# Attention and MLP block on one core: leftover parts of a half unit go to the next dense group, GpSimd's share of the normalisation written as a sum and a product, memsets and weight pieces spread out

## The chip, the cores and the metric

The kernel runs on one core of a Trainium2 chip. The metric is the device time of one execution in microseconds. Before the change it is 1500.49 us, the median of 3 runs (1500.31 to 1501.24).

## The reference

A transformer layer with both branches fed by the same normalised rows. 2048 rows of 512 numbers; 32 heads of 16; a hidden layer of 1792.

```
x  = A_x                                   # 1 x 2048 x 512, fp32
xn = (x - mean(x)) / sqrt(var(x) + 1e-5)   # per row
q, k, v = split(xn @ wqkv)                 # 32 heads of 16
p  = softmax(q k^T / 4)
out = x + (p v) @ wo + gelu(xn @ w1 + b1) @ w2 + b2
```

Everything is fp32 on the outside. Inside, an fp32 operand of a product is kept as two fp16 halves, high and low, and a product is made as three (high·high, high·low, low·high; `PAIRS` in the code). The exps and their product with v stay fp32.

## The kernel before

**Units.** The attention is cut into 512 units: 8 groups of 4 heads, 4 blocks of 512 query columns, 16 steps each. A unit has a score half and an exps half. The score half makes 4 tiles of scores (line 287, four products of 32x512 each, written side by side) and VectorE takes the row maximum of each tile (line 288). The exps half of the same unit comes 20 units later (`LEAD`), since it needs the maxima of all 16 steps: 4 products of q and k again with the maximum folded in (`e_half`), ScalarE's exp on each (line 339), and the fp32 products of the exps with v (`v_half`). So each pass through `unit()` does the score half of unit u and the exps half of unit u - 20.

**Dense work.** The fp32 products with v occupy one half of the rows of the array at a time, and the other half of the rows is given to what the code calls dense groups: sums of products that belong to the projections, the MLP or the output projection. A group is a list of products for each half of the array (side 0 and 1), an accumulation bank, and a `finish` that takes the result out. `dense(gen, side)` puts in so many *parts* (a part is 256 columns of a product; a full product of 512 columns is two) for each half unit, a number called the pace. The pace before is 8 parts for v groups, projections and 5 of 9 of the hidden groups (`FAST`), 6 for the other hidden groups (`SLOW`), and 7 for the groups of the second MLP product (`MEAN`). A hidden group has 24 parts a side, a sum group 42. Only one group is current (`cur[0]`, lane D), and when it ends in a half unit, the share that is left there is not used. A second lane, E, exists already, and is used at the very end only.

**Order of a run.** It is written out by hand at the start and then generated.
- *Start.* x comes in as 16 blocks of 128 rows. `stats(sb)` normalises four blocks: statistics on VectorE (lines 790 and 792), a short chain on `sd`, a 128x4 tile (lines 794 to 805), and then the normalisation of `xs` itself, which VectorE does for the first four blocks (line 815), and of the second four GpSimd for two (line 810), VectorE for one and ScalarE, in two passes, for one; GpSimd does all of the blocks from 8 on. TensorE transposes them (line 834), ScalarE, VectorE and GpSimd split the result into high and low (`xt`, line 842 for GpSimd), and `side(sb, w)` makes the first q and k projections (line 482). `prep_v` prepares v's weights: an absolute maximum on VectorE (line 751), then the split. `clear(i)` fills 16 stacks of q and k with GpSimd's memsets (lines 86 and 87); `clear(1)` stands in the start, ahead of GpSimd's first normalisation.
- *Units 0 to 15*, written as `scores(u, fills...)`: a score half whose spaces are filled with rows of v (`v_rows`, line 591: 12 products of 128x512 for each block of 128 rows), transposes, sides of the projection, and steps of `ms`, which measures the MLP weights by absolute sums on ScalarE (line 756). 9 of the 16 blocks of v are made here; 7 are left for later (`MOVED`).
- *Units 16 to 19* (`LEAD`) with `burst(LFILL)`, full-height products of the dense groups, 3 in each half unit.
- *Units from 20 on*: dense groups in the order v groups, projections of the other three quarters of the heads, hidden groups and sum groups by turns, and the output projection. After unit 511 the exps halves run on for 20 units, and then full-height products end the run.

**Beside it.** `prepare()` scales and splits the 16 pieces of w1, w2 and wo on GpSimd (lines 1038, 1039 and 1040), one piece after another as its queue comes free, and the split pieces go to DRAM. GpSimd's work in the units goes through `pooled`, a queue with an estimate of its load; DMAs and late steps go through `later(n)`, which runs a step n half or whole slots on. SyncE issues every DMA, in program order, so what stands behind a waiting DMA waits too. The loads of the q and k stacks (line 439) go there, and so do the steps of each query block's division: denominators out (line 377), back across partitions (line 380), a reciprocal on VectorE (line 383).

Of the kernel before, what the change touches and what calls it, by code (L numbers as in the profile page):

```python
# [24 lines left out]
NC = D // P  # L25
# [6 lines left out]
FAST, MEAN, SLOW, LATE = (8, 8), (7, 7), (6, 6), 6  # L32
MOVED = 7
# [4 lines left out]
LFILL = 3  # L38
# [11 lines left out]
def layer_kernel(ctx: ExitStack, tc: tile.TileContext, x, wqkv, wo, w1, b1, w2, b2, out):  # L50
# [32 lines left out]
    def clear(i):  # L83
        for b in range(NQB):
            for p in range(2):
                nc.gpsimd.memset(kst[i][p][b].bitcast(F32), MROW2)
                nc.gpsimd.memset(qst[i][p][b].bitcast(F32), 0.0)
# [76 lines left out]

    def split(hi, lo, src, inv):

        nc.scalar.activation(hi, src, AF.Copy, scale=inv)
        nc.vector.scalar_tensor_tensor(lo, src, inv, hi, op0=ALU.mult, op1=ALU.subtract)
# [274 lines left out]
    def dbank():  # L443
        turn[0] += 1
        if pos[0] < LEAD:
            return banks(free[turn[0] % len(free)]), None
# [6 lines left out]
    class Group:  # L453
# [3 lines left out]
        def __init__(self, prods, alloc, finish, ready=None, first=True, last=True, upper=None, pace=FAST):  # L457
# [87 lines left out]
    def project(m, w, sb, wh, bank, early=False, then=lambda: None):  # L545
# [6 lines left out]
        def finish(pj):  # L552
# [6 lines left out]
            if early or (w == 1 and not m):  # L559
# [17 lines left out]
        return Group(prods, bank, finish)  # L577
# [46 lines left out]
    def group(gen, lane=0):  # L624

        if cur[lane] is None and not spent[0]:
            cur[lane] = next(gen, 0)
            if cur[lane] == 0:
                cur[lane], spent[0] = None, True
        return cur[lane]  # L630

    def ended():

        for lane, f in enumerate(cur):
            if f is not None and f.over():
                cur[lane] = None
                f.end()

# [15 lines left out]
    def dense(gen, side, between=lambda: None):  # L654
# [28 lines left out]
    def unit(gen):  # L683
# [4 lines left out]
        if u == LEAD and cur[0] is not None:  # L688
            burst(gen, cur[0].left())
# [40 lines left out]
    with ExitStack() as st1:  # L730
# [55 lines left out]
        def stats(sb):  # L786
# [20 lines left out]
            for i in range(4):  # L807
                v = xs[4 * sb + i]
                if sb > 1 or (sb and i < 2):
                    nc.gpsimd.tensor_scalar(v, v, mv[:, i, 0:1], sd[:, 2, i:i + 1], op0=ALU.subtract, op1=ALU.mult)  # L810
# [534 lines left out]
```

## Time and profile before

| what | value |
|---|---|
| median of 3 runs | 1500.49 us |
| the profiled execution's own time | 1496.13 us |
| span of that execution | 1494.3 us |
| TensorE busy | 1442.6 us, 97% |
| VectorE busy | 1353.4 us, 91% |
| ScalarE busy | 1246.1 us, 83% |
| GpSimd busy | 763.2 us, 51% |
| mean granted clock of TensorE | 0.985 |

The span is what the trace covers; the profiled execution took 1.8 us more than that, and 4.4 us less than the median of the runs. Lines are those of the kernel before unless the text says otherwise. In a list of groups by line stands the operation, what it writes and reads, its tile, how many, the busy time and the mean of one in ns, and the idle time ahead of it with what ended that. In a table of windows stands for each stretch its length, the busy time of TensorE, its weight loads, VectorE, ScalarE and GpSimd (with counts), the granted clock, the busy share of the DMA engines and their GB/s; with a line given, it shows that line's engine alone. Since four maxima of line 288 make a unit, a quarter of their count is the number of units in a stretch.

### The profile page before, as it was taken

How to read it: one execution, taken by the hardware profiler on the slowest of the kernel's cores; microseconds unless marked ns; L12 is line 12 of the kernel's file. 1: busy time of each engine (PE TensorE's matmuls, PEld its weight loads, DVE VectorE, ACT ScalarE, POOL GpSimd, SP SyncE). 2: the span in 40 equal slices, each digit the busy share in tenths (PEclk: the TensorE clock that was granted, in tenths of full speed). 3: DMA queues.
4: the chain of work that ended last, by engine and by line, in shares of the span. 5: the costliest groups of instructions: out<-in, count | busy, mean ns of one | idle time of the engine just before them, and what ended most of it. 6: DMA issues, size and time to landing. Idle time of an engine off the chain costs nothing.

```text
span 1494.3 us, 89118 instructions
## 1 busy us (share of the span) xinstructions
PE 1442.6 (97%) x40674; PEld 945.1 (63%) x40674; DVE 1353.4 (91%) x2302; ACT 1246.1 (83%) x2383; POOL 763.2 (51%) x860
## 2 busy tenths in 40 slices
PE   6698989999999999999999999999999999999998
PEld 3234556667656666666666666666666666676675
DVE  6677989999999999999999999999999999999923
ACT  3256878888988999999999899999899989998874
POOL 5510288943477664665466375476556537541000
PEclk8899999999999999999999999999999999999999
DMA  5464166522332312112111211121111211002332
GB/s 187 125 181 136 56 203 223 185 78 94 103 118 70 88 37 65 34 58 62 51 37 62 78 29 38 44 73 52 57 44 48 69 41 51 16 23 85 111 125 97
DMA packets 117999, 124.50 MB, mean 83 GB/s; under 512 B 28920, under 2 KB 89592, under 8 KB 117620
## 3 DMA queue, kind: packets, MB, share of 16 engines
q1 hardware_dynamic: 117620, 118.79, 25.8%
q8 instruction: 318, 5.21, 1.4%
q14 instruction: 61, 0.50, 0.1%
HBM read 81.00 MB, written 37.60 MB: 79 GB/s over the span
## 4 chain that ended last, share of the span: by engine, by line
PE 88%; POOL 4%; DVE 3%; issue 2%; ACT 2%; DMA 1%; SPq 0%; DVEq 0%; POOLq 0%; ACTq 0%
PE pD L191 25%; PE pV L191 24%; PE pT L191 18%; PE pS L287 16%; PE pS L191 2%; POOL xs L810 1%; PE pT L591 1%; DVE mt L288 1%; ACT pe L339 1%; PE pS L482 0%; POOL t L1127 0%; DMA wq<-in_A_wqkv_dram 0%; POOL g L1129 0%; DMA wch<-in_B_w_dram 0%; POOL xt L842 0%
## 5 line engine op out<-in xcount | busy, mean ns | idle before, releaser
L288 DVE TENSOR_REDUCE mt<-pS 128x1 f32<-128x512 f32 x2048 | 1280.0, 683 | 62.6 <-PE pS L287 42.9
L339 ACT ACTIVATE pe<-pT 128x512 f32<-128x512 f32 x2048 | 1105.0, 598 | 149.0 <-PE pS L287 83.9
L191 PE MATMUL pV<-pe,vv 64*32 64x512 f32 x8192 | 1092.1, 597 | 3.1 <-issue 2.9
L191 PE MATMUL pT<-qst,kst 64*32 64x512 f16 x8192 | 677.2, 377 | 6.2 <-ACT pe L339 2.9
L287 PE MATMUL pS<-kst,qst 62*32 62x512 f16 x8192 | 614.3, 379 | 5.8 <-DVE mt L288 5.4
L191 PE MATMUL pD<-w_s,g 64*32 64x512 f16 (+1 forms) x6144 | 363.6, 348 | 0.1
L191 PE MATMUL pD<-xb,wc 64*32 64x512 f16 x5376 | 361.3, 375 | 0.0
L287 PEld LDWEIGHTS <-qst 62*32 62x32 f16 x8192 | 246.9, 92 | 124.7 <-issue 29.8
L191 PEld LDWEIGHTS <-kst 64*32 64x32 f16 x8192 | 255.0, 93 | 98.1 <-issue 20.8
L191 PEld LDWEIGHTS <-g 64*32 64x32 f16 x6144 | 198.3, 92 | 88.3 <-POOL g L1129 1.5
L191 PEld LDWEIGHTS <-wc 64*32 64x32 f16 x5376 | 174.8, 92 | 83.4 <-issue 0.4
L191 PEld LDWEIGHTS pV<-pe,vv 64*32 64x32 f32 x8192 | 181.1, 105 | 12.0 <-issue 6.8
L191 PE MATMUL pD<-xt,wqk_h 64*32 64x512 f16 x2400 | 161.3, 375 | 3.6 <-issue 3.6
L1156 POOL TENSOR_SCALAR hh<-hh,fac,b_s 128x512 f32<-128x512 f32 x56 | 43.0, 769 | 154.0 <-ACT hh L1154 150.4
L1183 POOL TENSOR_TENSOR xa<-xa,yt 128x512 f32<-128x512 f32 x32 | 41.0, 1283 | 141.4 <-ACT yt L1181 141.4
L191 PEld LDWEIGHTS <-wqk_h 64*32 64x32 f16 x2400 | 78.8, 92 | 36.9 <-issue 6.7
L394 POOL TENSOR_TENSOR osb<-osb,rb 128x512 f32<-128x512 f32 x31 | 39.9, 1286 | 84.9 <-DMA rb<-den_d 82.8
L1127 POOL TENSOR_TENSOR t<-t,hh 128x512 f32<-128x512 f32 x56 | 71.8, 1282 | 4.7
L1134 POOL TENSOR_TENSOR t<-t,hh 128x512 f32<-128x512 f32 x56 | 71.8, 1282 | 4.7
L1129 POOL TENSOR_TENSOR g<-t,g 128x512 f16<-128x512 f32 x56 | 65.2, 1164 | 4.7
L1132 POOL TENSOR_TENSOR t<-hh 128x512 f32<-128x512 f32 x56 | 58.2, 1040 | 4.7
L1220 DVE SCALAR_TENSOR_TENSOR ac<-pS,gs,ac 128x512 f32<-128x512 f32 x19 | 13.3, 746 | 50.0 <-PE pS L191 45.5
(153 smaller groups left out, 960.2 us busy)
## 6 DMA issues: line engine op xcount, KB each, us to landing
wch<-in_B_w_dram SPq DMA_DIRECT2D x28, 512.0 KB
wc<-w_d SPq DMA_DIRECT2D x56, 256.0 KB
qk_d<-stg SPq DMA_DIRECT2D x32, 256.0 KB
rb<-den_d SPq DMA_DIRECT2D x31, 256.0 KB
w_d<-wsp SPq DMA_DIRECT2D x28, 256.0 KB
kst<-qk_d SPq DMA_DIRECT2D x128, 48.0 KB
qst<-qk_d SPq DMA_DIRECT2D x128, 48.0 KB
xs<-in_A_x_dram SPq DMA_DIRECT2D x16, 256.0 KB
```

The costliest lines, as they stand in the source:

```text
L191: p = nc.tensor.matmul(*args, **kw)
L287: nc.tensor.matmul(s[32 * j:32 * j + 32], qs[p][qb][r, c:c + 32], ks[p][kb][r, :], start=True, stop=True)
L288: nc.vector.reduce_max(mt_of[t][:, n, qt, kb:kb + 1], s, axis=AX.X)
L339: nc.scalar.activation(pe, st, AF.Exp, scale=factor(exp_scale, sexp[0:1, g // 2:g // 2 + 1]))
L394: pooled((1280, lambda: nc.gpsimd.tensor_tensor(osb, osb, rb, op=ALU.mult)), (620, lambda: nc.gpsimd.tensor_scalar(ot[:, 0], osb, 1.0, 0.0 ...
L591: nc.tensor.matmul(pj, xt[:, i, c, t * P:(t + 1) * P], wh[j][:, c, :], start=(n == 0), stop=(n == 11))
L1127: (1280, lambda: nc.gpsimd.tensor_tensor(t1, t1, hh, op=ALU.mult)),
L1129: (1160, lambda: nc.gpsimd.tensor_tensor(g[:, 1, f, :], t1, g[:, 0, f, :], op=ALU.subtract)),
L1132: pooled((1040, lambda: nc.gpsimd.tensor_tensor(t1, hh, hh, op=ALU.mult)), (620, lambda: nc.gpsimd.tensor_scalar(t1, t1, 1.0, 1.0 / GELU_A ...
L1134: (1280, lambda: nc.gpsimd.tensor_tensor(t1, t1, hh, op=ALU.mult)),
L1156: later(1, lambda: pooled((690, lambda: nc.gpsimd.tensor_scalar(hh, hh, scale, bias, op0=ALU.mult, op1=ALU.add)), (0, lambda: gelu(hh, g, ...
L1183: add = lambda: nc.gpsimd.tensor_tensor(xa, xa, yt, op=ALU.add)
```

## The change

- **Hand-over.** `pace` is 8 for v groups and projections and 7 for everything else. When a group has nothing left for a side in a half unit, `dense` gives the rest of that half unit's parts to the next group, in the other lane; `lane[0]` says which lane is the current one. 680 products that were 512 columns wide become two of 256.
- **Front of the dense list.** `MOVED` goes from 7 to 6, so that 10 blocks of v are made by hand at the start; `LFILL` goes from 3 to 4; the burst that emptied the current group at unit 20 goes.
- **Normalisation.** GpSimd's form is (x + (-mean))·rstd instead of (x - mean)·rstd, with -mean in a column of `sd` that is there already. The fourth block of the second quarter goes from ScalarE to VectorE.
- **Memsets.** `clear(1)` is spread over units 7 to 15.
- **Order at the start.** The statistics of the second quarter stand ahead of v's absolute maximum on VectorE; 6 instead of 12 products of v stand ahead of unit 0; transposes, sides and stacks of the later quarters stand one or two units later. Sides (1,1), (2,1) and (3,1) are taken out by ScalarE and GpSimd instead of ScalarE and VectorE. The split of v's weights is in two steps.
- **Weight pieces.** Piece n isn't put in before 4·n units after the first.
- **Small moves.** The x of the next MLP block is fetched one slot later, the accumulators of the output projection earlier (`len(acs) - 2` instead of `2 + 2 * len(acs) - 6`).

```
@@ -29 +29 @@
 LEAD = 20
-FAST, MEAN, SLOW, LATE = (8, 8), (7, 7), (6, 6), 6
-MOVED = 7
+FAST, MEAN, LATE = (8, 8), (7, 7), 6
+MOVED = 6
...
 TAIL = 12
-LFILL = 3
+LFILL = 4
@@ -83 +83 @@
             for p in range(2):
+                yield
@@ -454 +448 @@
-        def __init__(self, prods, alloc, finish, ready=None, first=True, last=True, upper=None, pace=FAST):
+        def __init__(self, prods, alloc, finish, ready=None, first=True, last=True, upper=None, pace=MEAN):
@@ -556 +550 @@
             given("act", 600)
-            if early or (w == 1 and not m):
+            if early:
@@ -574 +568 @@
-        return Group(prods, bank, finish)
+        return Group(prods, bank, finish, pace=FAST)
@@ -621 +615 @@
-    def group(gen, lane=0):
-        if cur[lane] is None and not spent[0]:
-            cur[lane] = next(gen, 0)
-            if cur[lane] == 0:
-                cur[lane], spent[0] = None, True
-        return cur[lane]
+    lane = [0]
+    def group(gen, k=0):
+        if cur[k] is None and not spent[0]:
+            cur[k] = next(gen, 0)
+            if cur[k] == 0:
+                cur[k], spent[0] = None, True
+        return cur[k]
+    def busy():
+        return any(f is not None for f in cur)
...
-        for lane, f in enumerate(cur):
+        for k, f in enumerate(cur):
             if f is not None and f.over():
-                cur[lane] = None
+                cur[k] = None
                 f.end()
+        if cur[lane[0]] is None and cur[1 - lane[0]] is not None:
+            lane[0] = 1 - lane[0]
@@ -659 +660 @@
             return
-        f = group(gen)
-        n = 0 if f is None else f.pace[pos[0] % 2]
-        n = some_of(f, side, n, 0 if f is not None and f.ends(n) else BEHIND)
+        f = group(gen, lane[0])
+        if f is None:
+            between()
+            return
+        def share(n, until):
+            n = some_of(f, side, n, until)
+            if n > until and f.left(side) == 0 and (side == 0 or cur[1 - lane[0]] is not None):
+                g = group(gen, 1 - lane[0])
+                if g is not None and (n > 1 or g.at != [0, 0]):
+                    n = some_of(g, side, n, until)
+            return n
+        n = f.pace[pos[0] % 2]
+        n = some_of(f, side, n) if f.ends(n) else share(n, BEHIND)
         between()
-        some_of(f, side, n)
+        share(n, 0)
...
-        for lane, user in enumerate("DE"):
-            leave(user, cur[lane] is not None and not cur[lane].over())
+        for k, user in enumerate("DE"):
+            leave(user, cur[k] is not None and not cur[k].over())
...
             enter()
-            for lane, f in enumerate(cur):
-                while f is not None and f.left((k + lane) % 2):
-                    f.product((k + lane) % 2)
+            for i, f in enumerate(cur):
+                while f is not None and f.left((k + i) % 2):
+                    f.product((k + i) % 2)
@@ -685 +698 @@
         e = u - LEAD
-        if u == LEAD and cur[0] is not None:
-            burst(gen, cur[0].left())
@@ -807 +818 @@
                 if sb > 1 or (sb and i < 2):
-                    nc.gpsimd.tensor_scalar(v, v, mv[:, i, 0:1], sd[:, 2, i:i + 1], op0=ALU.subtract, op1=ALU.mult)
-                elif sb and i == 3:
-                    nc.scalar.activation(v, v, AF.Identity, bias=sd[:, 4, i:i + 1])
-                    nc.scalar.activation(v, v, AF.Copy, scale=sd[:, 2, i:i + 1])
+                    nc.gpsimd.tensor_scalar(v, v, sd[:, 4, i:i + 1], sd[:, 2, i:i + 1], op0=ALU.add, op1=ALU.mult)
@@ -865 +873 @@
             fac_v.append(fac)
-            for i in range(2):
-                cs = slice(i * W, (i + 1) * W)
-                split(wvh[0][:, :, cs], wvh[1][:, :, cs], wvf[i], inv[:, 0:1])
+            halves = [slice(i * W, (i + 1) * W) for i in range(2)]
+            for cs, v in zip(halves, wvf):
+                nc.scalar.activation(wvh[0][:, :, cs], v, AF.Copy, scale=inv[:, 0:1])
+            yield
+            for cs, v in zip(halves, wvf):
+                nc.vector.scalar_tensor_tensor(wvh[1][:, :, cs], v, inv[:, 0:1], wvh[0][:, :, cs], op0=ALU.mult, op1=ALU.subtract)
+                yield
@@ -945 +957 @@
         turn_all(0)
+        run(ln)
+        some(l1, 2)
         run(pq)
-        run(ln)
-        clear(1)
-        some(l1, 2)
-        some(pv, 1)
-        some(l1, 1)
+        some(l1, 4)
...
         run(l1)
+        some(pv, 1)
@@ -962 +973 @@
         free_banks["S"].append(free_banks["T"].pop(0))
-        ln, vs = stats(2), v_rows()
+        ln, vs, rest_0 = stats(2), v_rows(), clear(1)
         pj = side(1, 1)
-        for n in range(3):
-            some(pj, 4)
-            some(pv, 1)
+        some(pj, 4)
+        some(pv, 1)
+        some(ln, 1)
+        some(pj, 4)
+        some(pv, 1)
+        some(ln, 1)
+        some(pj, 3)
+        some(pv, 1)
+        some(ln, 2)
...
         run(pv)
-        some(ln, 5)
...
         run(ln)
-        some(vs, 12)
+        some(vs, 6)
         ln = stats(3)
-        scores(0, (vs, 3), (turn_x(2, 0), 1), (vs, 3), (turn_x(2, 1), 1))
-        for w in (1, 0):
-            stacks(0, w, [1])
+        scores(0, (vs, 10))
+        stacks(0, 1, [1])
+        scores(1, (vs, 3), (turn_x(2, 0), 1), (vs, 3), (turn_x(2, 1), 1))
         some(ln, 2)
-        scores(1, (vs, 3), (turn_x(2, 2), 1), (vs, 3), (turn_x(2, 3), 1))
+        scores(2, (vs, 3), (turn_x(2, 2), 1), (vs, 3), (turn_x(2, 3), 1))
         some(ln, 2)
-        scores(2, (side(2, 1), 13))
-        some(ln, 4)
         fetch(0)
-        scores(3, (side(2, 0), 13))
+        scores(3, (side(2, 1), 13))
         run(ln)
-        scores(4, (vs, 3), (turn_x(3, 0), 1), (ms, 1), (vs, 3), (turn_x(3, 1), 1))
-        for w in (1, 0):
-            stacks(0, w, [2])
-        scores(5, (vs, 3), (turn_x(3, 2), 1), (ms, 1), (vs, 3), (turn_x(3, 3), 1))
-        scores(6, (side(3, 1), 13), (ms, 1))
-        scores(7, (vs, 8), (ms, 1))
-        for u in range(8, 16):
-            scores(u, (vs, 4), (ms, 1), (vs, 4), (ms, 1))
-            if u == 8:
+        scores(4, (vs, 4), (ms, 1), (vs, 4))
+        stacks(0, 0, [1])
+        scores(5, (vs, 3), (turn_x(3, 0), 1), (ms, 1), (vs, 3), (turn_x(3, 1), 1))
+        stacks(0, 1, [2])
+        scores(6, (vs, 3), (turn_x(3, 2), 1), (ms, 1), (vs, 3), (turn_x(3, 3), 1))
+        scores(7, (side(3, 1), 13), (ms, 1), (rest_0, 2))
+        scores(8, (side(2, 0), 13), (ms, 2), (rest_0, 2))
+        for u in range(9, 16):
+            scores(u, (vs, 6 if u < 11 else 5), (ms, 1), (vs, 5), (ms, 1), (rest_0, 1))
+            if u == 9:
                 stacks(0, 1, [3])
-            elif u == 9:
                 wfs.append(load_qk(1))
+            elif u == 10:
+                stacks(0, 0, [2])
         run(vs)
+        run(rest_0)
@@ -1064 +1081 @@
             nc.vector.tensor_scalar_mul(gs[:, 1:2], gs[:, 1:2], 0.5)
-            ended = [True]
+            ended, first = [True], pos[0]
...
                 v = fetch(16 + n)
-                while not ended[0]:
+                while not ended[0] or pos[0] < first + 4 * n:
@@ -1157 +1174 @@
             return Group([lambda c=c, i=i, j=j: (wc[:, i, c, :], xb[:, j, c, :]) for c in range(NC) for i, j in PAIRS],
-                         dbank, hidden, pace=FAST if (HF * s + f) % 9 in (0, 2, 4, 6, 8) else SLOW)
+                         dbank, hidden)
@@ -1167 +1184 @@
             if q == 3 and s % 2 == 0:
-                fetch_x(b + 1)
+                later(1, lambda: fetch_x(b + 1))
@@ -1185 +1202 @@
             return Group([lambda f=f, i=i, j=j: (g[:, i, f, q * P:(q + 1) * P], w2_s[:, j, s % 2 * HF + f, :])
-                          for f in range(HF) for i, j in PAIRS], dbank, store, lambda n: (s, n // 3) in done, pace=MEAN)
+                          for f in range(HF) for i, j in PAIRS], dbank, store, lambda n: (s, n // 3) in done)
@@ -1278 +1295 @@
                     acs[k] = p3.tile([P, D], F32, name=f"ac{k}")
-                    later(2 + 2 * len(acs) - 6, lambda k=k: read_acc(acs[k], k))
+                    later(len(acs) - 2, lambda k=k: read_acc(acs[k], k))
```

VectorE at the start, where the second quarter is normalised (`mv` and `sd` the statistics, `xs` the rows, `stg` a side on its way out, `am_v` the maximum of v's weights); before:

```order
L792 BN_AGGR mv<-bs 128x2
L794 TENSOR_SCALAR sd<-mv 128x4
L751 TENSOR_REDUCE am_v<-wch 128x1
L798 TENSOR_SCALAR sd<-mv 128x4
L799 TENSOR_TENSOR sd<-sd 128x4
L561 TENSOR_TENSOR stg<-pS,stg 128x512
L801 TENSOR_TENSOR sd<-sd 128x4
L803 RECIPROCAL sd<-sd 128x4
L805 SCALAR_TENSOR_TENSOR sd<-sd 128x4
L815 TENSOR_SCALAR xs<-xs,mv,sd 128x512
```

and now:

```order
L803 BN_AGGR mv<-bs 128x2
L805 TENSOR_SCALAR sd<-mv 128x4
L524 TENSOR_TENSOR sexp<-fac_239 128x1
L525 TENSOR_SCALAR sexp<-sexp 128x1
L809 TENSOR_SCALAR sd<-mv 128x4
L810 TENSOR_TENSOR sd<-sd 128x4
L812 TENSOR_TENSOR sd<-sd 128x4
L814 RECIPROCAL sd<-sd 128x4
L816 SCALAR_TENSOR_TENSOR sd<-sd 128x4
L555 TENSOR_TENSOR stg<-pS,stg 128x512
L823 TENSOR_SCALAR xs<-xs,mv,sd 128x512 x2
L762 TENSOR_REDUCE am_v<-wch 128x1
```

The maximum of v's weights and the side's `stg` stood in the middle of the chain on `sd`, and stand behind it now; the block of xs that ScalarE normalised is VectorE's second.

GpSimd at the start, from the last of the memsets on; before:

```order
L86 MEMSET kst_1_3_97 128x256
L87 MEMSET qst_1_3_113 128x256
L810 TENSOR_SCALAR xs<-xs,mv,sd 128x512 x2
L842 TENSOR_TENSOR xt<-pf,xt 128x512 x2
L567 TENSOR_TENSOR stg<-pf,stg 128x512
L810 TENSOR_SCALAR xs<-xs,mv,sd 128x512 x4
L842 TENSOR_TENSOR xt<-pf,xt 128x512 x4
L567 TENSOR_TENSOR stg<-pf,stg 128x512
L810 TENSOR_SCALAR xs<-xs,mv,sd 128x512 x4
```

and now:

```order
L518 TENSOR_TENSOR wqk_h<-wq,wqk_h 128x512
L821 TENSOR_SCALAR xs<-xs,sd 128x512 x2
L850 TENSOR_TENSOR xt<-pf,xt 128x512 x2
L561 TENSOR_TENSOR stg<-pf,stg 128x512 x2
L821 TENSOR_SCALAR xs<-xs,sd 128x512 x4
L850 TENSOR_TENSOR xt<-pf,xt 128x512 x4
L561 TENSOR_TENSOR stg<-pf,stg 128x512
L821 TENSOR_SCALAR xs<-xs,sd 128x512 x4
```

The 16 memsets that stood between `wqk_h` and the first `xs` are gone from here, and one more `stg` stands ahead of the third quarter's `xs`.

GpSimd where the first weight pieces are split, after unit 20 (`wch` a piece, `wsp` its halves, `stg` a projection's result; the numbers tell the pieces apart); before:

```order
L1038 TENSOR_SCALAR wch_2950<-wch_2950,inv3_2660 128x2x4x128
L1039 TENSOR_SCALAR wsp_3155<-wch_2950 128x2x512
L1040 TENSOR_TENSOR wsp_3155<-wch_2950,wsp_3155 128x2x512
L1038 TENSOR_SCALAR wch_2952<-wch_2952,inv3_2660 128x2x4x128
L1039 TENSOR_SCALAR wsp_3353<-wch_2952 128x2x512
L1040 TENSOR_TENSOR wsp_3353<-wch_2952,wsp_3353 128x2x512
L569 TENSOR_SCALAR stg_3447<-pf_3448 128x512
L570 TENSOR_TENSOR stg_3447<-pf_3448,stg_3447 128x512
```

and now:

```order
L1055 TENSOR_SCALAR wch_2075<-wch_2075,inv3_2692 128x2x4x128
L1056 TENSOR_SCALAR wsp_2954<-wch_2075 128x2x512
L1057 TENSOR_TENSOR wsp_2954<-wch_2075,wsp_2954 128x2x512
L563 TENSOR_SCALAR stg_3048<-pf_3049 128x512
L564 TENSOR_TENSOR stg_3048<-pf_3049,stg_3048 128x512
L1055 TENSOR_SCALAR wch_2953<-wch_2953,inv3_2692 128x2x4x128
L1056 TENSOR_SCALAR wsp_3354<-wch_2953 128x2x512
L1057 TENSOR_TENSOR wsp_3354<-wch_2953,wsp_3354 128x2x512
```

Pieces that followed each other directly have a projection's `stg` between them now.

More of the change, by code (lines that the diff above doesn't have):

```diff
@@ L922, in layer_kernel @@
         nc.vector.memset(wvh[0][:, 0, :], 0.0)
-        clear(0)
+        run(clear(0))
         ln, l1, pq, pv = stats(0), stats(1), prep_qk(0, wfs[0], sbank, ready_w), prep_v()
@@ L1100, in layer_kernel @@
         fil, pre, more = rest(), prepare(), True
-        while not spent[0] or more or cur[0] is not None:
+        while not spent[0] or more or busy():
             unit(fil)
@@ L1253, in layer_kernel @@
         fil, spent[0] = mlp(), False
-        while not spent[0] or cur[0] is not None:
+        while not spent[0] or busy():
             more_stacks()
```

9 lines of the change are left out of this document (2 added, 7 removed).

## The prediction

> **What bounds the kernel now.** First the page: the busy time by engine (share of the span, instructions), and the chain of work that ended last, by engine.
>
> ```profile
> PE 1442.6 (97%) x40674; PEld 945.1 (63%) x40674; DVE 1353.4 (91%) x2302; ACT 1246.1 (83%) x2383; POOL 763.2 (51%) x860
> PE 88%; POOL 4%; DVE 3%; issue 2%; ACT 2%; DMA 1%; SPq 0%; DVEq 0%; POOLq 0%; ACTq 0%
> ```
>
> TensorE bounds it, so only two kinds of gain exist: less work on TensorE, or less waiting by it. The chain leaves TensorE for 12% of the span, with 4% on GpSimd. The windows over all engines show where TensorE waits.
>
> ```profile
> 42.50:56.30 13.80, 5.87 (x47) 2.47 (x46) 4.42 (x11) 3.22 (x8) 10.53 (x6) 0.67 0.37 115
> 56.30:68.40 12.10, 11.55 (x100) 4.62 (x89) 10.95 (x25) 5.02 (x11) 4.58 (x4) 0.95 0.25 66
> 68.40:80.20 11.80, 4.91 (x30) 2.05 (x27) 2.45 (x5) 2.24 (x6) 9.44 (x6) 0.62 0.66 213
> 80.20:111.80 31.60, 30.63 (x276) 11.52 (x269) 27.70 (x46) 18.57 (x51) 3.47 (x3) 0.98 0.66 194
> 180.00:300.00 120.00, 112.37 (x3247) 73.78 (x3236) 107.69 (x181) 96.51 (x182) 98.16 (x87) 1.00 0.64 201
> 320.00:385.00 65.00, 65.00 (x1990) 45.81 (x1979) 63.77 (x104) 58.01 (x110) 17.98 (x23) 1.00 0.28 87
> 480.00:1380.00 900.00, 899.17 (x27342) 613.33 (x27332) 880.96 (x1465) 816.22 (x1551) 503.66 (x567) 1.00 0.18 52
> ```
>
> From 480 to 1380 us TensorE is full (899.17 of 900), so the even pace has little to win there. Two stretches of the hand-written start stand out: TensorE idles 13.80 - 5.87 = 7.93 and 11.80 - 4.91 = 6.89 us, GpSimd is busy, and the granted clock falls to 0.67 and 0.62. The third place is 180 to 300 us. Counting the maxima of line 288, four to a unit, gives its pace.
>
> ```profile
> 180.00:300.00 120.00, 102.37 (x162) 1.00 0.64 201
> 320.00:385.00 65.00, 63.25 (x100) 1.00 0.28 87
> 189.70:220.00 30.30, 22.80 (x36) 1.00 0.71 217
> 245.60:300.30 54.70, 48.43 (x76) 1.00 0.58 184
> ```
>
> 180 to 300 us: 162/4 = 40.5 units at 2.96 us; 320 to 385 us: 25 at 2.60. The weight pieces cost 40.5 x 0.36 = 14.7 us.
>
> **A: up to unit 0.** The second quarter's normalisation, in the timeline of several engines:
>
> ```profile
> 17.71 2.22 DVE L794 TENSOR_SCALAR sd<-mv 128x4 f32<-128x4 f32 x1
> 42.26 0.17 DVE L794 TENSOR_SCALAR sd<-mv 128x4 f32<-128x4 f32 x1
> 19.60 0.31 POOL L87 MEMSET qst<- 128x256 f32 x1
> 21.98 4.38 POOL L810 TENSOR_SCALAR xs<-xs,mv,sd 128x512 f32<-128x512 f32 x2 [2.07 <-DVE sd L805]
> 24.36 0.47 PE L834 MATMUL pT<-ident,xs 128*128 128x128 f32 x1 [4.43 <-POOL xs L810]
> ```
>
> The same small operation on `sd` takes 2.22 us here and 0.17 later; here it ends at 19.93, with the last memset (19.91). With the memsets gone: -2.05. The next price is GpSimd's normalisation. The trace has no sum-and-product on `xs`; the nearest row is line 1156, a product and a sum with two columns on a tile of the same size.
>
> ```profile
> L810 POOL TENSOR_SCALAR xs<-xs,mv,sd 128x512 f32<-128x512 f32 x10 | 20.9, 2098 | 2.4 <-DVE sd L805 2.4
> L1156 POOL TENSOR_SCALAR hh<-hh,fac,b_s 128x512 f32<-128x512 f32 x56 | 43.0, 769 | 154.0 <-ACT hh L1154 150.4 <-DMA kst<-qk_d 3.5
> 39.82 2.75 PE L591 MATMUL pT<-wvh,xt 128*128 128x512 f16 x12
> 67.28 1.16 POOL L567 TENSOR_TENSOR stg<-pf,stg 128x512 f16<-128x512 f32 x1 [5.16 <-ACT stg L566]
> ```
>
> I take 0.77 for 2.10, bounded by no change on one side; nothing in the trace suggests less than 0.77. Two of them: 4.38 - 1.54 = -2.84. Six products of v leave the front: 6 x 2.75/12 = -1.4. Against it: VectorE gets another block, and a side now passes through GpSimd (1.16 each); I put +0.8 for what of that isn't covered by TensorE's own projections. A = -2.05 - 2.84 - 1.4 + 0.8 = -5.5. TensorE's first wait for `xs` alone is 4.43, nearly the first two terms together, so they can be had. Range -4 (half of GpSimd's gain) to -6.3 (no +0.8).
>
> **B: units 0 to 15.** Both idle stretches belong to GpSimd's groups of four.
>
> ```profile
> 44.85 8.24 POOL L810 TENSOR_SCALAR xs<-xs,mv,sd 128x512 f32<-128x512 f32 x4
> 68.72 8.24 POOL L810 TENSOR_SCALAR xs<-xs,mv,sd 128x512 f32<-128x512 f32 x4 [0.28 <-DVE sd L805]
> ```
>
> Four take 4 x 0.77 = 3.1 instead of 8.24, which is -5.2 twice; the later place of transposes and sides, with rows of v ahead of them, covers the rest. So the 14.8 us of idle time go, but the sides that now leave through GpSimd (1.16 each, two of them near the third and fourth quarters) can hold up `xs` or `xt`: I leave 2.3. Added: 18 products of v (6 from the front, 12 for the tenth block), 18 x 0.229 = +4.1. Clock: full clock would make 5.87 and 4.91 shorter by 0.33 x 5.87 + 0.38 x 4.91 = 3.8; I take half, since some waits stay: -1.9. The 16 memsets (16 x 0.31 = 5 us) now lie under units 7 to 15, where GpSimd is busy 3.47 of 31.6: nothing. B = -14.8 + 2.3 + 4.1 - 1.9 = -10.3. Range -6 (waits of 6.6 remain) to -13 (no waits, full clock).
> The Trainium skill (TensorE: Matmul & The Clock Gate, Part 1: The HAM clock gate) says that the clock is either half or full, dropping after an idle window of about 3.4 us and returning after about as long of sustained work. The rows agree with a fall after idleness (0.67 and 0.62, against 0.95 between them); as no idle window of that length would remain, the rule would give the whole 3.8, and B = -12.2.
>
> **C: units 16 to 20.** Here ScalarE must finish measuring before the exps start, and its last pieces stand on SyncE behind the maxima of the first block.
>
> ```profile
> 113.57 0.37 SPq L317 DMA_DIRECT2D m_d<-mhl  x1
> 118.01 0.38 SPq L745 DMA_DIRECT2D wch<-in_B_w_dram  x1
> 122.28 0.63 ACT L756 ACTIVATE wch<-wch 128x512 f32<-128x512 f32 x1 [5.46 <-DMA wch<-in_B_w_dram]
> ```
>
> The chain (maxima stored after unit 15, then load, then measure) keeps its order and moves with unit 15. The eight extra products that `LFILL` puts into units 16 to 19 are v's, which otherwise stand later, and fall where TensorE waits for ScalarE anyway: 0, +/-2.
>
> **E: weight pieces.** Pieces now stand 4 units apart at least, 4 x 2.6 = 10.4 us.
>
> ```profile
> 245.00:300.00 55.00, 17.15 (x8) 1.00 0.59 185
> 400.00:415.00 15.00, 15.00 (x452) 9.72 (x437) 14.46 (x24) 14.20 (x29) 8.98 (x10) 1.00 0.46 140
> 216.06 0.39 PE L191 MATMUL pD<-xt,wqk_h 64*32 64x512 f16 x1 [2.06 <-issue]
> ```
>
> The first row is line 1040: 8 pieces in 55 us, 6.9 apart, at a DMA share of 0.59. Spaced, the 0.31 above the quiet 0.28 shrinks to 0.31 x 6.9/10.4 = 0.21, a share of 0.49. At 0.46 (second row, all engines) TensorE has no gap; at 0.58 a unit is 0.28 longer (54.70/19 = 2.88), at 0.71 0.77 longer (30.30/9). On a straight line from 0.46 to 0.58 a share of 0.49 leaves 0.07, and 0.51 would leave 0.12; on 16 x 4 = 64 units that is 4.5 to 7.7 us of the 14.7. Loads of stacks still come in bunches on top, and the gap in the last row is put down to "issue", not to a DMA; so I halve the gain of 7 to 10 to E = -4, range 0 to -9.
>
> **F: unit 123.** The division of a query block comes late (its first DMA stands behind loads of stacks on SyncE's queue) and holds VectorE, then TensorE:
>
> ```profile
> 418.67 0.56 SPq L377 DMA_DIRECT2D den_d<-osb  x1
> 423.48 0.34 DVE L383 RECIPROCAL dn<-dn 64x32 f32<-64x32 f32 x1 [3.21 <-DMA dn<-den_d]
> 424.42 0.40 PE L287 MATMUL pS<-kst,qst 62*32 62x512 f16 x4 [2.88 <-DVE mt L288]
> ```
>
> The MLP, and with it the loads of stacks, begins 4 units earlier, so SyncE is clear by then: -2.88, less a chance that the maxima at unit 116 now queue behind them. F = -2.5, range -3.4 to +1.
>
> **G: pace.** Three windows of line 288, with 12, 16 and 14 parts a half unit:
>
> ```profile
> 594.20:604.20 10.00, 9.74 (x16) 1.00 0.16 44
> 637.70:653.40 15.70, 15.29 (x24) 1.00 0.18 56
> 1306.40:1382.90 76.50, 74.49 (x120) 1.00 0.18 53
> L191 PEld LDWEIGHTS <-wc 64*32 64x32 f16 x5376 | 174.8, 92 | 83.4 <-issue 0.4
> L191 PE MATMUL pD<-w_s,g 64*32 64x256 f16 x1536 | 113.8, 269 | 0.0
> ```
>
> Per unit (both halves together) 2.50, 2.62 and 2.55: 14 parts lie 0.01 under the mean of 12 and 16. On the 56 hidden groups, 56 x 48/14 = 192 units, that makes -1.5; I take G = -1, range -3 to +3, because the 680 products cut in two add 680 weight loads of 0.092. Sum groups have 1536 products of 256 columns already and lie on the line (the third window), so a loaded weight is hidden there.
>
> **H: end.** One group of the output projection moves behind unit 531:
>
> ```profile
> 1480.18 2.76 PE L482 MATMUL pS<-wo_s,oc 128*128 128x512 f16 x12
> 1487.32 0.60 PE L482 MATMUL pS<-wo_l,ot 64*128 64x512 f16 x2 [0.68 <-ACT ot L425]
> ```
>
> Of another 2.76 some covers the wait of 0.68, and as much dense work is gone from the units ahead: H = +1, range 0 to +2.
>
> **The sum.** -5.5 - 10.3 + 0 - 4 - 2.5 - 1 + 1 = -22.3. Against the profiled execution's own 1496.1: 1473.8. The runs' median stands 4.4 above that; I carry it along: 1500.5 - 22.3 = 1478.2.
>
> **Rivals.**
> R2, spacing pays nearly all: E = -13 in place of -4. For it: 320 to 385 us is free of gaps at a low share. Against: projections' own loads remain. 1469.
> R3, spacing pays nothing: "issue" gaps don't come from the DMA load. 1478.2 + 4 = 1482. The Trainium skill (Runtime: NRT & Kernel Launch, Instruction fetch mechanics) says that engines prefetch their instructions in sequence and that this is mostly hidden; by that rule the gaps aren't fetches held up by transfers, and the spacing saves nothing. The trace speaks against: gaps at shares of 0.58 to 0.71, none at 0.28 and 0.46.
> R4, the start gives it back: units 0 to 15 become limited by the loads that ScalarE measures. The first four windows move 13.8 x 115 + 12.1 x 66 + 11.8 x 213 + 31.6 x 194 kB, 11.0 MB in 69.3 us. In 59 us that is 187 GB/s, below the 213 of the third window, so it should fit; if not, some 12 of the 15.8 in A and B return: 1490.
> R5, slower: a hand-over inside a half unit shows its weight loads. All 680 x 0.092 = 62.6 us; the 22.3 are gone at 36% of that, and from 40% on the kernel is slower by over 0.2% (1503.5). Against: the sum groups' 1536.
> R6, no change: unit 20 is pinned by the loads and everything up to it is lost, with E at 0: 1500.5 - 2.5 = 1498.
>
> **Chances.** Forecast 0.62, R2 0.13, R3 0.10, R4 0.08, R5 0.05, R6 0.02. 0.2% is 3 us, about what a measurement of this kernel can tell from no change. Faster: 0.93; same: 0.02; slower: 0.05. The range reaches from R2 with a somewhat better start, 1465, to R4, 1490; beyond lie R5, R6 and the edges of the others.
>
> **What would show it.** In the profile after: `xs` on GpSimd at about 0.77 us (at 2.1, A and B lose 13); `sd` at 0.17; TensorE's idle time between units 0 and 8 under 4 us; ScalarE's last wait for `wch` ending near 106.5 (122.28 - 15.8); units under the pieces near 2.75; no wait at unit 123; 2.55 to 2.57 in the steady stage. Wrong would be a wait by ScalarE for `wch` longer than 5.46, or steady units over 2.60.

## The result and the profile after

The changed kernel takes 1477.78 us, the median of 4 executions (1476.26 to 1482.32), against 1500.87 (1500.31 to 1501.29) beside it: a ratio of 0.9851, 95% interval 0.9829 to 0.9874, 23.1 us less. 1478.2 was forecast.

The two profiled executions lie 13.8 us apart, not 23: the changed kernel's is the slowest of its four (1482.32), and that of before (1496.13) is faster than its other ones. A table by stages is therefore read with that in mind. The limits are the starts of units, each taken at the first of its four maxima in the trace.

| stretch | before | after | difference | forecast |
|---|---|---|---|---|
| up to unit 0 | 43.4 | 34.4 | -9.0 | A -5.5 |
| units 0 to 16 | 68.4 | 54.7 | -13.7 | B -10.3 |
| units 16 to 24 | 26.9 | 25.7 | -1.2 | C 0 |
| units 24 to 107 | 238.0 | 239.9 | +1.9 | E -4 |
| units 107 to 128 | 57.2 | 60.7 | +3.5 | F -2.5 |
| units 128 to 496 | 946.5 | 951.5 | +5.0 | G -1 |
| unit 496 to the end | 113.9 | 113.6 | -0.3 | H +1 |

So the total hides misses that cancel: the start gave 22.7 in place of 15.8, and the stretches from unit 107 to 496 took 8.5 us where 3.5 were to be saved. The page of the changed kernel, busy times and the chain by engine:

```profile
PE 1444.5 (98%) x41162; PEld 942.6 (64%) x41162; DVE 1350.4 (91%) x2300; ACT 1248.2 (84%) x2384; POOL 752.7 (51%) x863
PE 88%; DVE 4%; ACT 2%; issue 2%; DMA 2%; POOL 1%; SPq 1%; DVEq 0%; POOLq 0%; ACTq 0%
```

GpSimd's share of the chain falls from 4% to 1%, which fits a gain that comes from there; the first two experiments price it. Its normalisation, the chain on `sd` and the first transposes after it, from the list by line and then the timeline of the changed kernel:

```profile
L821 POOL TENSOR_SCALAR xs<-xs,sd 128x512 f32<-128x512 f32 x10 | 7.7, 784 | 3.8 <-DVE sd L816 3.8
```

```profile
17.92 0.17 DVE L805 TENSOR_SCALAR sd<-mv 128x4 f32<-128x4 f32 x1
20.98 0.33 PE L842 MATMUL pT<-ident,xs 128*128 128x128 f32 x1 [0.16 <-POOL xs L821]
35.83 3.01 POOL L821 TENSOR_SCALAR xs<-xs,sd 128x512 f32<-128x512 f32 x4
```

One block takes 0.784 us (0.77 was taken), four 3.01; the operation on `sd` is at 0.17, and TensorE's wait of 4.43 for `xs` is 0.16. What the forecast had too small is in the windows over all engines (for each stretch its length, then the busy time of TensorE, its weight loads, VectorE, ScalarE and GpSimd, the granted clock, the DMA share and GB/s): two stretches of before that weren't shown, up to unit 0 and from there to unit 16,

```profile
14.80:43.40 28.60, 20.65 (x94) 9.97 (x94) 17.85 (x44) 9.79 (x19) 11.80 (x21) 0.76 0.37 112
43.40:111.80 68.40, 52.33 (x414) 20.41 (x414) 44.93 (x82) 28.15 (x70) 28.02 (x18) 0.85 0.54 161
```

and the same two of the changed kernel:

```profile
14.80:34.40 19.60, 15.31 (x90) 7.36 (x90) 17.77 (x45) 9.43 (x18) 7.07 (x7) 1.00 0.50 153
34.40:89.10 54.70, 50.00 (x431) 20.55 (x430) 44.33 (x81) 29.21 (x72) 23.84 (x36) 0.97 0.71 208
```

In the first stretch TensorE's idle time falls by 3.7 us, and its busy time by 5.3 with four matmuls less, as its granted clock goes from 0.76 to 1.00. In the second its idle time falls from 16.1 to 4.7 us, and its busy time by 2.3 although 17 matmuls are added. That the same work takes less time is seen on the transposes of `xs`, 16 in the first stretch and 32 in the second. Their line alone (TensorE and its weight loads), before,

```profile
14.80:43.40 28.60, 3.94 (x16) 3.14 (x16) 0.76 0.37 112
43.40:111.80 68.40, 8.03 (x32) 5.15 (x32) 0.85 0.54 161
```

and in the changed kernel:

```profile
14.80:34.40 19.60, 2.13 (x16) 1.79 (x16) 1.00 0.50 153
34.40:89.10 54.70, 5.13 (x32) 4.05 (x32) 0.97 0.71 208
```

The wait at unit 123 is gone: that unit takes 2.68 us (5.96 before). In its place stands one at unit 116. SyncE's queue and then TensorE, in the timeline of the changed kernel, and the window after it:

```profile
369.20 3.26 SPq L435 DMA_DIRECT2D qst<-qk_d  x4
372.56 0.37 SPq L616 DMA_DIRECT2D wc<-w_d  x1
372.98 1.84 SPq L435 DMA_DIRECT2D qst<-qk_d  x4
374.92 1.34 SPq L313 DMA_DIRECT2D m_d<-mhl  x1
377.59 2.61 SPq L318 DMA_DIRECT2D qst<-m_d  x4
380.14 0.62 PE L187 MATMUL pT<-qst,kst 64*32 64x512 f16 x4 [3.14 <-DMA qst<-m_d]
```

```profile
380.00:393.00 13.00, 12.74 (x304) 6.98 (x312) 9.10 (x15) 8.95 (x18) 6.03 (x8) 0.77 0.48 143
```

The maxima stand behind loads of stacks on SyncE, TensorE waits 3.14 us for them, and comes back at a lower clock: 0.77 over the next 13 us. From maximum to maximum unit 115 takes 6.13 us and unit 116 4.91, where a unit takes some 2.55: 5.9 us in all.

### The profile page after: what moved, and what is told of

Same layout as the page of the kernel before. It is cut to its first block, busy times and chain, and to the rows that moved or that the text cites. A ratio compares the mean times of both kernels' runs of the same rounds, so it can differ in the third digit from the quotient of the medians.

```text
span 1480.5 us, 90088 instructions
## 1 busy us (share of the span) xinstructions
PE 1444.5 (98%) x41162; PEld 942.6 (64%) x41162; DVE 1350.4 (91%) x2300; ACT 1248.2 (84%) x2384; POOL 752.7 (51%) x863
## 4 chain that ended last, share of the span: by engine, by line
PE 88%; DVE 4%; ACT 2%; issue 2%; DMA 2%; POOL 1%; SPq 1%; DVEq 0%; POOLq 0%; ACTq 0%
PE pD L187 26%; PE pV L187 23%; PE pT L187 18%; PE pS L283 16%; DVE mt L284 2%; PE pS L187 2%; PE pT L585 1%; ACT pe L335 1%; DMA wch<-in_B_w_dram 1%; DVE ac L1237 0%; PE pT L476 0%; DMA rb<-den_d 0%; PE pS L476 0%; DMA wq<-in_A_wqkv_dram 0%; POOL xs L821 0%
## 5 line engine op out<-in xcount | busy, mean ns | idle before, releaser
L283 PE MATMUL pS<-kst,qst 62*32 62x512 f16 x8192 | 632.6, 380 | 6.3 <-DVE mt L284 4.2
L187 PE MATMUL pD<-xb,wc 64*32 64x512 f16 (+1 forms) x6056 | 367.9, 352 | 0.0
L187 PE MATMUL pD<-w_s,g 64*32 64x512 f16 x6136 | 366.1, 348 | 0.2
L187 PEld LDWEIGHTS <-kst 64*32 64x32 f16 x8192 | 263.1, 93 | 128.8 <-issue 43.8
L283 PEld LDWEIGHTS <-qst 62*32 62x32 f16 x8192 | 238.8, 92 | 111.2 <-issue 33.4
L187 PEld LDWEIGHTS <-g 64*32 64x32 f16 x6136 | 193.1, 92 | 86.6 <-issue 1.8
L187 PEld LDWEIGHTS <-wc 64*32 64x32 f16 x6056 | 191.0, 92 | 84.9 <-issue 2.0
L307 POOL TENSOR_SCALAR mrow<-mrow 128x32 f32<-128x32 f32 x32 | 6.9, 217 | 142.9 <-DVE mrow L304 142.8
```

What stands on the lines that cost most here:

```text
L187: p = nc.tensor.matmul(*args, **kw)
L283: nc.tensor.matmul(s[32 * j:32 * j + 32], qs[p][qb][r, c:c + 32], ks[p][kb][r, :], start=True, stop=True)
```

## The experiments

Three questions: what part of the start's gain is the form of GpSimd's operation; whether spacing, hand-over and the wait at unit 116 cost or pay what the trace suggests; and what the changed kernel would be without its losses. The theory that came out of the traces (S in the expectations: the start is nearly all of the gain) stands against the forecast's own sum (P).

**The form alone.** On the kernel before, in one line:

```
-nc.gpsimd.tensor_scalar(v, v, mv[:, i, 0:1], sd[:, 2, i:i + 1], op0=ALU.subtract, op1=ALU.mult)
+nc.gpsimd.tensor_scalar(v, v, sd[:, 4, i:i + 1], sd[:, 2, i:i + 1], op0=ALU.add, op1=ALU.mult)
```

> The kernel before with one edit: GpSimd normalises as a sum and a product. Theory S (the start is nearly all of the gain, and GpSimd's form is its largest part): xs takes 0.75 to 0.8 us in place of 2.1, TensorE's two idle stretches of 7.9 and 6.9 us lose about 5 us each and the wait before the second quarter's transposes 2 to 3; 11 to 13 us less than before, 1488 to 1490. Rival O (the order of the start is the larger part, since statistics, memsets and the split of v's weights are next late): 5 us or less, 1495 or more.

Measured: 1486.04 us (ratio 0.9896, 0.9863 to 0.993), unit 16 at 97.8 in place of 111.8. Its list by line, and its window from unit 0 to unit 16:

```profile
L810 POOL TENSOR_SCALAR xs<-xs,sd 128x512 f32<-128x512 f32 x10 | 7.8, 795 | 2.3 <-DVE sd L805 2.3
```

```profile
39.50:97.80 58.30, 52.20 (x414) 20.70 (x414) 44.98 (x83) 28.24 (x70) 17.58 (x18) 0.91 0.63 189
```

In the two profiled executions one line of code brings unit 16 forward by 14.0 us, where the whole change brings it forward by 22.7. Theory S, and a little more than it expected.

**The difference again, with the sum's operands.** On the changed kernel, the mean with its sign in the column tile:

```
-nc.vector.tensor_scalar_mul(sd[:, 4], mv[:, :, 0], -1.0)
+nc.vector.tensor_scalar_mul(sd[:, 4], mv[:, :, 0], 1.0)
...
-nc.gpsimd.tensor_scalar(v, v, sd[:, 4, i:i + 1], sd[:, 2, i:i + 1], op0=ALU.add, op1=ALU.mult)
+nc.gpsimd.tensor_scalar(v, v, sd[:, 4, i:i + 1], sd[:, 2, i:i + 1], op0=ALU.subtract, op1=ALU.mult)
```

> The changed kernel with GpSimd's normalisation as a difference and a product again, but with its mean from the same column tile that the sum reads. Theory A (GpSimd is slow at the difference itself): xs 2.06 us each, unit 16 at 97 to 103 in place of 89, 1486 to 1490. Theory B (it was slow at the mean's place in memory, columns two apart in mv): xs 0.75 us, 1478 as the changed kernel.

Measured: 1494.83 us (ratio 0.9954, 0.9931 to 0.9977), unit 16 at 106.6. Its list by line, and its window from unit 0 to unit 16:

```profile
L821 POOL TENSOR_SCALAR xs<-xs,sd 128x512 f32<-128x512 f32 x10 | 20.6, 2073 | 4.9 <-DVE sd L816 4.9
```

```profile
39.00:106.60 67.60, 54.38 (x439) 21.70 (x432) 44.36 (x80) 29.22 (x71) 34.24 (x36) 0.87 0.58 167
```

Same tiles, same columns, 2.073 us: what GpSimd is slow at here is the difference in place of the sum, not where the mean lies. Theory A; the cost to the kernel is larger than it expected. From both sides the form is worth about the same: 1 - 0.9896 is 15.6 us of 1500, 0.9954 - 0.9851 is 15.5, with intervals of some 3 to 5 us on either side.

**The memsets back in the start.** `run(clear(1))` stands ahead of the second quarter's normalisation again, and `rest_0` is empty.

> The changed kernel with the 16 memsets in the start again, ahead of GpSimd's first normalisation. If the small operation on sd waits for the row of memsets (2.22 us before): it waits again 1.5 to 2.2 us, and units 0 and 16 begin 2 to 3 us later, 1480 to 1481. Rival: the wait is covered, since TensorE has the first quarter's projections to do: unit 0 at 34 to 36, 1478.

Measured: 1482.16 us, but spread from 1469.99 to 1485.48 (ratio 0.9839, 0.9798 to 0.9879, which holds the changed kernel's). In the timeline the wait is back:

```profile
17.68 2.48 DVE L805 TENSOR_SCALAR sd<-mv 128x4 f32<-128x4 f32 x1
19.82 0.32 POOL L88 MEMSET qst<- 128x256 f32 x1
22.15 0.33 PE L842 MATMUL pT<-ident,xs 128*128 128x128 f32 x1 [2.00 <-POOL xs L821]
```

The operation on `sd` ends at 20.16, with the last memset at 20.14, and TensorE waits 2.00 us in place of 0.16. Unit 0 begins at 37.4. Over the other executions with the same start it begins at 34.1 to 37.8, so the wait is shown, and its worth in the total is not: inconclusive there.

**The start alone.** The changed kernel with the old dense schedule (paces of 8 and 6, no hand-over) and the pieces close together; the small moves and the front of the dense list stay as changed:

```
-FAST, MEAN, LATE = (8, 8), (7, 7), 6
+FAST, MEAN, SLOW, LATE = (8, 8), (7, 7), (6, 6), 6
...
-            if n > until and f.left(side) == 0 and (side == 0 or cur[1 - lane[0]] is not None):
-                g = group(gen, 1 - lane[0])
-                if g is not None and (n > 1 or g.at != [0, 0]):
-                    n = some_of(g, side, n, until)
...
-                         dbank, hidden)
+                         dbank, hidden, pace=FAST if (HF * s + f) % 9 in (0, 2, 4, 6, 8) else SLOW)
...
-                while not ended[0] or pos[0] < first + 4 * n:
+                while not ended[0]:
```

> The changed kernel with the old dense schedule (hidden groups at 8 and 6 parts, no hand-over) and no spacing of the weight pieces; what is left is the start, with 10 blocks of v and 4 products a half unit in units 16 to 19. Theory S: unit 16 begins at 89 us as in the changed kernel, the rest runs as before or a few us better than in the changed kernel, 1472 to 1478. Theory P (the sum as predicted: start 15.8, spacing 4, pace 1): 1482 to 1485.

Measured: 1472.78 us (1470.13 to 1476.45; ratio 0.9833, 0.9792 to 0.9874). Theory S: by the medians the start is worth as much as the whole change, and the intervals (the whole change has 0.9829 to 0.9874) show no gain from the rest taken together. Its units 140 to 496 take 913.7 us; the changed kernel's take 920.6.

**Stacks in every other unit.** On the changed kernel:

```
-        if g + 2 < NG and pos[0] - LEAD >= 64 * (g + 1) + 3:
+        if g + 2 < NG and pos[0] % 2 and pos[0] - LEAD >= 64 * (g + 1) + 3:
```

> The changed kernel with the loads of stacks in every other unit. Theory Q (the 3.1 us wait at unit 116 is the maxima's DMAs queued on SyncE behind those loads, and the half clock after it doubles it): no wait at unit 116, units 115 and 116 at 2.5 to 2.7 in place of 6.1 and 4.9, 3 to 6 us faster than the changed kernel, 1472 to 1475. Rival: the wait is the way of the maxima itself (transpose, GpSimd, DRAM and back), which the earlier MLP makes visible: unchanged, 1478.

Measured: 1473.81 us (1472.28 to 1474.94; ratio 0.9832, 0.9795 to 0.987). SyncE's queue in its timeline, and its window from unit 107 to 128 for the maxima's line, under the changed kernel's:

```profile
366.94 0.38 SPq L313 DMA_DIRECT2D m_d<-mhl  x1
368.52 2.61 SPq L318 DMA_DIRECT2D qst<-m_d  x4
```

```profile
352.47:406.61 54.14, 51.98 (x85) 1.00 0.41 122
```

```profile
354.66:415.35 60.69, 52.28 (x85) 0.94 0.36 109
```

The maxima go out at once and no unit waits for them: 6.5 us less in this stretch. Theory Q. A second set of executions on another chip gave 1472.49 (below).

Over all traces of kernels with the new start, the stretch takes 53.8 to 55.3 us where the stacks' loads are apart, and 55.4 (old dense schedule) and 57.3 to 60.7 where they are not, so 6.5 is the largest difference that the traces hold. TensorE's wait for the maxima there is 1.43, 2.55, 3.14, 3.40 and 3.44 us. What follows differs: behind 3.14 us the granted clock was 0.77 over 13 us, behind 3.44 it was 0.87, and behind 3.40, in the run with the difference again, it stayed full:

```profile
391.10:404.10 13.00, 12.83 (x386) 7.97 (x394) 11.71 (x19) 11.40 (x22) 8.56 (x11) 1.00 0.51 145
```

**Without the spacing.** The changed kernel with `while not ended[0]:` again:

> The changed kernel with the weight pieces as close as before. Theory S, in which the spacing moves the same cost about: within 2 us of the changed kernel's 1478. Theory P: 4 us slower, 1482. Rival R2 (spacing pays nearly all of 14.7): 1491.

Measured: 1482.33 us, spread from 1477.52 to 1488.88 (ratio 0.9889, 0.9851 to 0.9927): it leans to theory P, but its interval overlaps the changed kernel's. Since this and the dense schedule are sizes of a few us, they were measured again beside a common neighbour.

**Three neighbours on one chip.** The changed kernel with the old dense schedule and the stacks apart, spacing kept (first run by itself):

> The changed kernel with the old dense schedule (8 and 6 parts, no hand-over), and with the stacks in every other unit; the spacing stays. Theory H (units in which two groups share take 0.10 us more, and the halved products lengthen the units of sums by 0.02): units 140 to 496 take about 914 us in place of 919 to 920 as in the run with stacks apart, and the whole is 4 to 5 us faster than that run's 1474: 1469. Rival: the even pace gains what the hand-over costs, and the 5 us are noise between executions: 1474.

Measured: 1468.0 us (ratio 0.9762, 0.9742 to 0.9782); theory H. Then again, with two neighbours, one without the spacing and one with the new dense schedule (even pace and hand-over together):

> The kernel with the old dense schedule, spacing and stacks apart again, beside its neighbours on one chip: 1466 to 1470, all theories.

> The same without the spacing of the weight pieces. Theory P (spacing pays 4 us, as the pair with and without it under the new dense schedule had it in one execution each, 239.9 and 244.3 us for units 24 to 107): 1471 to 1473 and some 4 us more in units 24 to 107. Theory S (nothing: the old dense schedule has 239.8 without and 241.4 with it): within 2 us of its neighbour.

> The changed kernel with stacks apart (new dense schedule with hand-over) beside the one with the old dense schedule. Theory H: 4 to 5 us slower than it, 1472 to 1475, and units 140 to 496 some 4 to 5 us longer. Rival: the same time within 2 us.

| kernel (6 executions each) | median | range | ratio to before |
|---|---|---|---|
| old dense schedule, stacks apart, spaced | 1466.98 | 1463.27 to 1471.99 | 0.9772 (0.9746 to 0.9798) |
| the same, pieces close | 1474.67 | 1469.41 to 1477.88 | 0.9811 (0.9783 to 0.984) |
| new dense schedule, stacks apart, spaced | 1472.49 | 1469.3 to 1476.51 | 0.9802 (0.9776 to 0.9828) |

The medians say 7.7 us for the spacing and 5.5 for the old dense schedule against the new one; by the means of six it is 6.9 and 5.8, with 95% about +/-4.0 and +/-3.6 from the spread of the sets. The windows of the maxima's line, units 24 to 107 and then 140 to 496, for the first kernel:

```profile
113.91:349.66 235.75, 210.83 (x332) 1.00 0.49 148
433.75:1349.20 915.45, 887.65 (x1424) 1.00 0.18 52
```

with the pieces close,

```profile
116.00:360.81 244.81, 210.26 (x333) 0.99 0.48 142
445.75:1360.59 914.84, 887.78 (x1425) 1.00 0.18 52
```

and with the new dense schedule:

```profile
116.13:353.45 237.32, 210.65 (x333) 0.99 0.51 147
440.33:1359.16 918.83, 885.46 (x1424) 1.00 0.18 52
```

In these traces the spacing acts in units 24 to 107 (244.8 to 235.8) and not in units 140 to 496, and the dense schedule acts there (915.5 to 918.8). The first pair of traces is a wide draw: the spaced execution (1463.27) is the fastest of its six. The second holds in every trace: units 140 to 496 take 913.7 to 915.5 us in the four kernels with the old dense schedule and the new start, and 918.8 to 920.6 in the six with the new one. Theory S falls on the spacing, which costs more than theory P expected when it is left out; theory H on the dense schedule. The first of the three is the best kernel found: it takes the changed kernel's start and spacing, and neither its hand-over nor its loads of stacks.

## Why the prediction was right, and where its terms were not

**The number.** 1478.2 against 1477.78 is a sum of errors of both signs, and that they cancel to 0.4 us is luck. Start and C gave -23.9 in the pair of traces, the spacing -4 to -8, unit 123 -3.3, unit 116 about +4 by the medians of the runs, and the dense schedule +3 to +6.

**A, right in mechanism, too small (-5.5, measured -9.0).** All three steps happened: 2.10 to 0.78 us a block, 2.22 to 0.17 on `sd`, the wait of 4.43 gone. The waits were sized rightly: -2.05 - 2.84 + 0.8 = -4.1, and TensorE's idle time fell by 3.7. The term left out is the clock: the granted clock up to unit 0 was 0.76, and TensorE's busy time there falls by 5.3 us, where -1.4 was put for products of v. The same 16 transposes alone take 1.8 us less. The forecast priced the clock in B only, where its rows had been looked at.

**B, the same (-10.3, measured -13.7).** The waits fell by 11.4 us, where 14.8 - 2.3 = 12.5 were taken. The missed size is TensorE's busy time, which fell by 2.3 where +4.1 - 1.9 = +2.2 was put. With 17 more products at the forecast's 0.229 (+3.9) that leaves some 6.2 us, an estimate, for work that ran faster at a clock of 0.97 in place of 0.85; half of 3.8 was taken, and the 3.8 itself covered only the work inside the two idle stretches. The same 32 transposes alone take 2.9 us less. Here the Trainium skill's rule (TensorE: Matmul & The Clock Gate, Part 1: The HAM clock gate), by which the whole loss goes once no idle window is left, was the better guide: it made B -12.2. The waits at unit 116 lie near its window of about 3.4 us, and the traces go both ways there: 3.14 us was followed by 0.77 over 13 us, 3.40 us by 1.00.

**C, right** (0, +/-2; -1.2).

**E, right in sign and range (-4, range 0 to -9), not in its working.** In the profiled pair it looks like +1.9, since 238.0 is a quick draw of a kernel with close pieces: the other executions with close pieces that have a trace show 239.6, 239.8, 244.3 and 244.8, those of spaced kernels 235.8 to 241.4 and once 233.3. The means of these five and seven lie 3.6 us apart, and the paired runs give -6.9 +/-4.0; the forecast is near the one and inside the other. R3, and with it the consequence drawn from the Trainium skill's Instruction fetch mechanics (Runtime: NRT & Kernel Launch) that spacing saves nothing, falls. The working went over the DMA share: 0.49 was to come, and units of 2.75 us. The windows of the maxima's line from the first piece's unit to the last one's, before and in the changed kernel:

```profile
169.19:297.28 128.09, 108.79 (x172) 1.00 0.62 192
148.20:330.86 182.66, 162.33 (x257) 1.00 0.53 156
```

Before, 43 units take 2.98 us each at a share of 0.62; now 64 take 2.85 at 0.53. Above the quiet 2.60 that is 16.3 us both times, so the straight line from share to length doesn't hold in this pair. That the "issue" gaps are fetches behind data is argued only: no run here separates it from another cause.

**F, wrong in sign (-2.5, measured +3.5).** The wait at unit 123 went, as said. The step that failed is the price of the risk at unit 116: the forecast named it and bounded F at +1. It became 3.14 us of waiting, nearly doubled by the clock in this execution. The stacks' loads had moved 4 units earlier, from under one query block's division to under another's maxima: the wait was exchanged, not removed.

**G, wrong in sign (-1, measured +5.0).** At the old paces a group ended exactly with a half unit (24 parts are 3 x 8 or 4 x 6, 42 are 6 x 7), so in the steady stage no share was left unused; only the even pace of 7, which doesn't divide 24, leaves one to hand over. The even pace itself gained little, as the straight line said: units with parts of hidden groups alone take 2.57 us, against 2.57 as the mean of those with 12 and 16. The loss lies around the ends of groups. In units 140 to 496, each taken from its first score product to the next one's, the first and the third of the three neighbours compare like this:

| units 140 to 496 | old dense schedule | new |
|---|---|---|
| a group ends in it | 80 at 2.61 us | 43 that two groups share at 2.67, 37 others at 2.56 |
| the one after such a unit | 80 at 2.55 | 80 at 2.62 |
| the others | 196 at 2.56 | 196 at 2.55 |

The units with an end cost about the same as before on the mean (2.61 and 2.62). The unit after the end, which the forecast didn't look at, costs 0.07 more: some 5.7 us, of which the others give back 2.8; the whole comes to the 3.4 us by which the two windows above differ. R5's mechanism, the weight loads of halved products, isn't what is seen. From the run with stacks apart, TensorE in a shared unit, and its products from 535.75 to 536.08 apart by shape:

```profile
535.25 0.40 PE L187 MATMUL pT<-qst,kst 64*32 64x512 f16 x4
535.71 0.63 PE L187 MATMUL pV<-pe,vv 64*32 64x512 f32 x4
535.76 0.51 PE L187 MATMUL pD<-xb,wc 64*32 64x256 f16 x8
536.09 0.40 PE L187 MATMUL pD<-w_s,g 64*32 64x512 f16 x4
536.30 0.40 PE L187 MATMUL pD<-w_s,g 64*32 64x512 f16 x4
536.52 0.40 PE L283 MATMUL pS<-kst,qst 62*32 62x512 f16 x4
536.59 0.73 PE L187 MATMUL pT<-qst,kst 64*32 64x512 f16 x8
537.14 0.61 PE L187 MATMUL pV<-pe,vv 64*32 64x512 f32 x4
```

```profile
L187 PE MATMUL pD<-xb,wc 64*32 64x512 f16 x4 | 0.4, 374 | 0.0
L187 PE MATMUL pD<-xb,wc 64*32 64x256 f16 x4 | 0.3, 267 | 0.0
```

The timeline puts operations that follow each other on one tile into one row, so the row of eight is four products of 256 columns and four of 512. They hold the place for 0.33 us (535.76 to 536.09), and the four of 512 behind them, on the sum group, for 0.21 (536.09 to 536.30): the four of 256 take what is left, about half, and halving costs nothing there. The lost time of this unit stands later, inside the row of `pT`: from 536.52 to 537.14 the scores' and exps' products take 0.62 us, where they take 0.46 from 535.25 to 535.71. The second four of `pT` begin at 536.92, behind the two exps that ScalarE ends at 536.88:

```profile
535.79 1.09 ACT L335 ACTIVATE pe<-pT 128x512 f32<-128x512 f32 x2 [0.19 <-PE pS L283]
```

Why the order of a shared unit makes TensorE meet the exps too early, and whether the same wait makes up all of the 0.07 in the units after, stays open; the even pace and the hand-over weren't tried one without the other.

**H, right** (+1; -0.3). **The rivals.** R2 (spacing -13) and R4 (start given back) didn't come; ScalarE's last wait for `wch` is 2.29 us and ends at 99.49, where 5.46 was the limit (an earlier one, at 72.10, is 5.09). R6 didn't either. **The other signs.** TensorE idles 2.5 us between units 0 and 8 (under 4 was said). The steady units take 2.59 us where 2.55 to 2.57 was said, and stay under the 2.60 that would have been wrong.

## What to carry to other kernels

Price a wait of TensorE with the granted clock of the stretch around it, before and after, and not by the idle time alone; a wait of some 3 us can go either way (0.77 behind 3.14 us, 1.00 behind 3.40). When a stretch of work moves, look at which transfer it will stand in front of at its new place, and give that the price of the one that it frees. An operation that looks equal on paper (a difference for a sum) is worth a row of its own in the list by line. Before paying for the sharing of what is left over, see whether the old sizes leave anything over.

## What the runs showed of the hardware that was not expected

- GpSimd's `tensor_scalar` with two columns on 128x512 fp32 takes 2.07 us as a difference and a product, and 0.78 to 0.80 us as a sum and a product; the columns were the same in the run with the difference again (2.073 and 0.784).
- A 128x4 operation on VectorE ran 2.22 and 2.48 us, ending with GpSimd's row of memsets, where it takes 0.17 with nothing on GpSimd beside it. It isn't the memsets alone: for the third quarter the changed kernel has it at 0.91 us, from 32.49 to 33.40, beside an operation on `stg` of GpSimd's that ends at 33.38.
- Repeated executions of one kernel differ by 1 to 16 us here, mostly more than the kernels' steady stages do (913.7 to 915.5 us for units 140 to 496 in four executions of the old dense schedule with the new start). In the traces the stretch that varies most is that of the weight pieces, units 24 to 107: 233.3 to 241.4 us over the kernels with spaced pieces.
